# Keys in natural order, a bias band, direct value loads and a new load order in an attention and FFN kernel

## The chip, the cores and the metric

The kernel runs on one core of one Trainium2 chip. The metric is the device time of one execution in microseconds (us). Engines: PE is TensorE (matmuls), PEld its weight loads, DVE is VectorE, ACT is ScalarE, POOL is GpSimd, SP is SyncE. "SPq" and "POOLq" are the instruction streams of SyncE and GpSimd when they issue DMA transfers.

## The reference, cut to what matters

```python
B, H, S, D = 8, 8, 576, 64                       # batch, heads, sequence, head size
scores = q @ k.transpose(0, 1, 3, 2) / sqrt(D)
n      = abs(pos[:, None] - pos[None, :])
bucket = where(n < 16, n, min(16 + int(15 * log(n / 16) / log(8)), 31))   # 31 from n = 128 on
scores = scores + bias_table[bucket].transpose(2, 0, 1)
attn   = softmax(scores) @ v                     # [B, H, S, D]
x      = attn as [4608 tokens, 512]
out    = ((x @ w_a) * (x @ w_b)) @ w_out         # 512 -> 1536 -> 512
```

Inputs and output are float32. The kernel computes in bf16. The bias depends on the distance alone, and it is constant beyond a distance of 128, so `exp(score + bias)` is `exp(score)` times a factor that is 1 outside a band around the diagonal once the last bucket's bias is subtracted.

## The kernel before

The work is 32 steps of two heads each (a "pair"; four pairs make a batch). A step computes scores on TensorE, exponentiates on ScalarE, multiplies by the bias factors on VectorE, and multiplies by v on TensorE. From step 4 on, the FFN's matmuls are woven into the steps. The 512 main rows of a sequence are four blocks of 128; the last 64 rows are "tails" with loads of their own. In batches 0 and 1, TensorE transposes q and k; from batch 2 on, four DMA transposes issued by SyncE do it (QTb, KTb and two for tails). Step 8 is the first that uses KTb.

All loads that convert float32 to bf16 are issued by GpSimd, in program order. They rotate over eight semaphores, so that a load cannot be issued before the one eight places earlier has landed; in the trace each such issue waits on its own semaphore.

```python
def load4(src, dst, b, h0, h1):              # v: runs of four rows, rows permuted (p t)
    nc.gpsimd.dma_start(
        out=dst[:, 256 * h0:256 * h1].rearrange("p (h x) -> p h x", x=256),
        in_=src[b, h0:h1, 0:SM, :].rearrange("h (p t) d -> p h (t d)", t=NM))

def load_t(src, dst, b, h0, h1, natural):    # q, k: one load per block of rows
    for t in range(NM):                      # NM = 4
        rows = slice(128 * t, 128 * t + 128) if natural else slice(t, SM, NM)
        nc.gpsimd.dma_start(out=dst[...][:, t, h0:h1, :],
                            in_=src[b, h0:h1, rows, :].transpose([1, 0, 2]))

def v_in(b, h0, h1):                         # vn -> vm, which has a column of ones per head
    nc.vector.tensor_copy(out=vm[b % 2][:, h0:h1, :, 0:Dh], in_=vn[b % 2][...])

def mul(p, t):                               # bias factors for all 2 x 512 elements
    at, w = st[p]["at", t], W_sb[p % 4]
    nc.vector.tensor_tensor(out=at[:, :, :], in0=at[:, :, :],
                            in1=w[:, :, S - 1 + t:S - 1 + t - SM:-1], op=MULT)

# ... start: tails, q and k of heads 2 and 3, v, q and k of heads 4 to 7, ...
load_w(nc.gpsimd, 2); load_v(0, 4, 8); load_w(nc.gpsimd, 3)
load_w_in(0)                                 # first third of w_a and w_b
# ... end of step 0:
load_q(1, 0, 8); load_k(1, 0, 8); load_tails(1)
load_w_in(1); load_v(1, 0, 4); load_vt(1)
load_w_in(2); load_v(1, 4, 8)
load_w_out()
# ... end of step 4:
load_qkt(2)                                  # q, k and tails of batch 2
```

The softmax here doesn't subtract the row's maximum and nothing guards it: scores larger than these inputs give would overflow.

## Time and profile before

| | us |
|---|---|
| median of three runs, before the prediction | 437.79 (437.36 to 437.79) |
| span of the profiled execution | 436.25 |
| first exp of the attention (ScalarE) | 11.21 |
| last tails of batch 1 landed | 36.02 |
| first FFN matmul | 46.26 |
| w_out landed | 58.40 |
| KTb of batch 2 landed / first used | 76.4 / 84.05 |

The first two lines below are the page of the kernel before: busy time of each engine with its share of the span, and the granted TensorE clock in tenths over 40 equal slices (9 is 90% or more). The third, from the page as well, is the chain of work that ended last, by engine.

```profile
PE 418.2 (96%) x3349; PEld 206.1 (47%) x3349; DVE 235.2 (54%) x529; ACT 244.6 (56%) x346; POOL 103.5 (24%) x139
PEclk8595999999999999999999999999999999999999
PE 89%; DMA 5%; POOL 3%; DVE 2%; issue 1%; ACT 0%; DVEq 0%; POOLq 0%
```

TensorE is 96% busy, and it is 89% of the chain. Half clock lies within the first four slices (the clock records say 8.1 to 21.8 and 32.0 to 42.3 us). The next view is the busy time by window, with the columns of its first line; GB/s is what the transfers moved.

```profile
core 0: us, PE busy (x) PEld busy (x) DVE busy (x) ACT busy (x) POOL busy (x), PEclk, DMA share, GB/s
20.00:30.00 10.00, 8.97 (x134) 6.38 (x132) 8.69 (x25) 9.00 (x13) 6.62 (x8) 0.91 1.64 202
30.00:40.00 10.00, 7.01 (x61) 4.42 (x61) 3.56 (x11) 3.71 (x6) 8.59 (x13) 0.60 1.70 159
100.00:400.00 300.00, 300.00 (x2391) 145.24 (x2390) 162.51 (x348) 174.40 (x249) 37.67 (x49) 1.00 0.58 80
```

In the 300 us from 100 to 400, TensorE is busy for 300.00 us at clock 1.00. So there is little in this stretch that less VectorE work could shorten. Only the first 80 us hold idle TensorE time. The largest waits of TensorE (list of waits: line that waits, what it waited for, total us, times, longest):

```profile
PE tab_ps L221 <- DMA oh_sb<-oh_const: 3.4, 1, 3.4
PE trq L276 <- DMA qn<-in_q_dram: 2.8, 5, 0.7
```

Finally the timeline of SyncE around the transposes of batch 2, and of TensorE where step 8 begins (start, duration, then the instruction; for a DMA the duration is that of its issue):

```profile
66.29 4.74 SPq L312 DMA_TRANSPOSE KTb<-kn  x1
84.05 0.61 PE L327 MATMUL qk<-QTb,KTb 64*128 64x512 bf16 x4
```

The transpose was issued at 66.29 us and its data landed at 76.4 us. It was used at 84.05 us, without a wait. The last load of its k is the eighth after w_out in GpSimd's program:

```profile
39.10 1.07 POOL L166 DMA_DIRECT2D wo<-in_moe_w_out_dram  x1
58.93 0.89 POOL L127 DMA_DIRECT2D kn<-in_k_dram  x1 [7.17 <-PE pa L446]
```

### The profile page before, as it was taken

What the parts mean: (1) busy time and instruction counts of PE and PEld (TensorE: products, weight loads), DVE (VectorE), ACT (ScalarE), POOL (GpSimd) and SP (SyncE); (2) the same over time, 40 slices, a digit from 0 to 9 for tenths busy, and PEclk for the clock granted to TensorE, in tenths of its full rate; (3) what the DMA queues carried; (4) which work ended last, traced back from release to release, by engine and by line L of the source; (5) the groups of instructions that cost most, each with busy time, mean ns of one, the idle gap of its engine ahead of it and who ended that gap; (6) DMA issues with size and microseconds to landing.
All of it is one profiled execution on the core that took longest, in us unless ns stands there. A gap on an engine that the chain in (4) does not pass through costs nothing.

```text
span 436.2 us, 8373 instructions
## 1 busy us (share of the span) xinstructions
PE 418.2 (96%) x3349; PEld 206.1 (47%) x3349; DVE 235.2 (54%) x529; ACT 244.6 (56%) x346; POOL 103.5 (24%) x139
## 2 busy tenths in 40 slices
PE   5978998999999999999999999999999999999995
PEld 2455554554444444444545444444444454444442
DVE  3674767665764576456655575466636651321320
ACT  1875665657665666566656665666566633223321
POOL 9966547290009000720063001000000000000000
PEclk8595999999999999999999999999999999999999
DMA  9999999999249925994579562431021002002004
GB/s 125 205 177 171 200 164 188 140 130 183 52 56 109 226 41 64 90 184 101 63 63 193 106 76 38 131 73 39 15 86 38 15 20 81 0 19 79 0 4 94
DMA packets 145863, 41.87 MB, mean 96 GB/s; under 512 B 127608, under 2 KB 141080, under 8 KB 145824
## 3 DMA queue, kind: packets, MB, share of 16 engines
q0 software_dynamic: 90864, 19.21, 51.7%
q1 hardware_dynamic: 53760, 21.79, 24.2%
q8 instruction: 26, 0.43, 0.4%
q10 hardware_dynamic: 1200, 0.33, 0.4%
q14 instruction: 13, 0.11, 0.1%
HBM read 39.22 MB, written 9.45 MB: 112 GB/s over the span
## 4 chain that ended last, share of the span: by engine, by line
PE 89%; DMA 5%; POOL 3%; DVE 2%; issue 1%; ACT 0%; DVEq 0%; POOLq 0%
PE pb L456 23%; PE po L466 22%; PE pa L446 22%; PE av L400 9%; PE qk L327 7%; DMA qn<-in_q_dram 2%; PE av L391 2%; PE qkt L349 1%; DMA vt<-in_v_dram 1%; PE qkt L352 1%; POOL qn L127 1%; DMA qtl<-in_q_dram 1%; PE trx L429 1%; DVE g L459 0%; DVE at L343 0%
## 5 line engine op out<-in xcount | busy, mean ns | idle before, releaser
L338 ACT ACTIVATE at<-qk 128x1024 bf16<-128x1024 f32 x128 | 126.8, 1025 | 28.5 <-PE qk L327 28.1
L459 DVE TENSOR_TENSOR g<-pb,ha 128x512 bf16<-128x512 f32 x108 | 74.7, 692 | 102.0 <-PE pb L456 90.6
L446 PE MATMUL pa<-xn,wa 128*128 128x512 bf16 x432 | 111.1, 379 | 0.0
L456 PE MATMUL pb<-xn,wb 128*128 128x512 bf16 x432 | 110.9, 379 | 0.0
L450 ACT ACTIVATE ha<-pa 128x512 f32<-128x512 f32 x108 | 64.5, 598 | 72.6 <-PE pa L446 72.5
L466 PE MATMUL po<-wo,g 128*128 128x512 bf16 x432 | 102.5, 379 | 0.0
L343 DVE TENSOR_TENSOR at<-at,W 128x1024 bf16<-128x1024 bf16 x128 | 86.0, 685 | 9.2 <-ACT at L338 8.9
L456 PEld LDWEIGHTS <-wb 128*128 128x128 bf16 x432 | 38.8, 97 | 53.0 <-issue 17.2
L446 PEld LDWEIGHTS <-wa 128*128 128x128 bf16 x432 | 38.8, 98 | 49.8 <-issue 10.3
L466 PEld LDWEIGHTS <-g 128*128 128x128 bf16 x432 | 38.4, 98 | 45.9 <-issue 7.6
L470 ACT ACTIVATE ob<-po 128x512 f32<-128x512 f32 x36 | 21.5, 597 | 68.3 <-PE po L466 68.3
L400 PE MATMUL av<-vm,at 128*128 128x65 bf16 x1024 | 48.5, 197 | 0.2 <-DVE vm L318 0.2
L400 PEld LDWEIGHTS <-at 128*128 128x128 bf16 x1024 | 43.9, 100 | 6.9 <-issue 0.3
L408 DVE RECIPROCAL rc<-av 128x6 f32<-128x6 f32 x64 | 12.1, 189 | 46.9 <-PE av L400 44.8
L391 PE MATMUL av<-vt,att 128*128 128x130 bf16 x160 | 35.6, 223 | 0.0
L409 DVE TENSOR_TENSOR XG<-av,rc 128x384 bf16<-128x384 f32 x64 | 31.4, 491 | 2.4 <-DVE rc L408 0.2
L363 ACT ACTIVATE att<-qkt 128x1024 bf16<-128x1024 f32 x32 | 32.6, 1020 | 0.0
L127 POOL DMA_DIRECT2D kn<-in_k_dram x32 | 27.9, 907 | 12.8 <-PE pa L446 8.8
L127 POOL DMA_DIRECT2D qn<-in_q_dram x32 | 27.7, 885 | 6.4 <-PE trq L276 5.7
L327 PE MATMUL qk<-QTb,KTb 64*128 64x512 bf16 x192 | 29.1, 381 | 0.0
L120 POOL DMA_DIRECT2D vn<-in_v_dram x10 | 8.6, 857 | 70.7 <-DVE vm L318 69.2
L148 POOL DMA_DIRECT2D vt<-in_v_dram x16 | 10.0, 638 | 60.1 <-PE av L400 60.0
(79 smaller groups left out, 243.3 us busy)
## 6 DMA issues: line engine op xcount, KB each, us to landing
out_dram<-ob SPq DMA_DIRECT2D x32, 256.0 KB, 2.3
qn<-in_q_dram POOLq DMA_DIRECT2D x28, 128.0 KB, 6.6
kn<-in_k_dram POOLq DMA_DIRECT2D x28, 128.0 KB, 9.2
vn<-in_v_dram POOLq DMA_DIRECT2D x6, 512.0 KB, 6.7
wa<-in_moe_w_a_dram POOLq DMA_DIRECT2D x3, 512.0 KB, 9.3
wb<-in_moe_w_b_dram POOLq DMA_DIRECT2D x3, 512.0 KB, 10.5
wo<-in_moe_w_out_dram POOLq DMA_DIRECT2D x1, 1536.0 KB, 19.3
vn<-in_v_dram POOLq DMA_DIRECT2D x4, 256.0 KB, 7.5
```

The lines of the kernel that those rows point to most:

```text
L127: nc.gpsimd.dma_start(out=dst[b % 2][:, :].rearrange("p (t h d) -> p t h d", h=H, t=NM)[:, t, h0:h1, :], in_=src[b, h0:h1, rows, :].transp ...
L327: nc.tensor.matmul(out=ps[:, hh, :], lhsT=kT_(p, t)[r, :], rhs=qT[r, :, :], start=True, stop=True)
L338: nc.scalar.activation(out=at[:, :, :], in_=ps[:, :, :], func=ACTF.Exp, scale=scale)
L343: nc.vector.tensor_tensor(out=at[:, :, :], in0=at[:, :, :], in1=w[:, :, S - 1 + t:S - 1 + t - SM:-1], op=MULT)
L363: nc.scalar.activation(out=at[:, ST:ST + 1024].rearrange("p (a x) -> p a x", a=2), in_=ps[:, :, :], func=ACTF.Exp, scale=scale)
L391: nc.tensor.matmul(out=pav[:, slot, :, :], lhsT=x, rhs=vt[i][:, hp, :, :], start=True, stop=True)
L400: nc.tensor.matmul(out=pav[:, slot, hh, :], lhsT=x, rhs=vm[i][:, 2 * hp + hh, t, :], start=False, stop=True, skip_group_check=True)
L446: nc.tensor.matmul(out=pa[:, :], lhsT=wa_sb[df // 4][:, mc, 128 * (df % 4):128 * (df % 4) + 128], rhs=xn_sb[mc][:, 512 * c:512 * c + 512], ...
L450: nc.scalar.activation(out=ha[:, :], in_=pa[:, :], func=ACTF.Copy)
L456: nc.tensor.matmul(out=pb[:, :], lhsT=wb_sb[df // 4][:, mc, 128 * (df % 4):128 * (df % 4) + 128], rhs=xn_sb[mc][:, 512 * c:512 * c + 512], ...
L459: nc.vector.tensor_tensor(out=g_sb[df][:, :], in0=pb[:, :], in1=ff["ha"][:, :], op=MULT)
L466: nc.tensor.matmul(out=po[:, :], lhsT=g_sb[df][:, 128 * tt:128 * tt + 128], rhs=wo_sb[:, df, :], start=(df == 0), stop=(df == NDF - 1))
```

## The change

The intent is fourfold. Keys stay in natural order, so the bias differs from 1 only on a band of 384 columns; VectorE multiplies 2 x 384 or 2 x 256 elements instead of 2 x 512. Values go straight into the tile that the matmul reads, so VectorE's copies disappear; their packets shrink from 512 to 128 bytes. The first transposes are split to start the first exp earlier. The loads are cut into smaller pieces and put in the order in which they are needed. The diff, cut to its core:

```diff
-    def load_t(src, dst, b, h0, h1, natural):
+    def load_t(src, dst, b, h0, h1):
         for t in range(NM):
-            rows = slice(128 * t, 128 * t + 128) if natural else slice(t, SM, NM)
             nc.gpsimd.dma_start(
-                in_=src[b, h0:h1, rows, :].transpose([1, 0, 2]))
+                in_=src[b, h0:h1, 128 * t:128 * t + 128, :].transpose([1, 0, 2]))
+    def load_p(src, dst, b, hp):                 # q or k of one pair: one load per head
+        for h in (2 * hp, 2 * hp + 1):
+            load_h(nc.gpsimd, src, x[:, :, h, :], b, h)
+    def load_v(b):                               # all heads, one load per block of rows
+        for t in range(NM):
+            nc.gpsimd.dma_start(out=vm[b % 2][:, :, t, 0:Dh], in_=v[b, :, 128*t:128*t+128, :]...)
+    def load_vp(b, hp):                          # v of one pair: one load per head
+        for h in (2 * hp, 2 * hp + 1):
+            load_h(nc.gpsimd, v, vm[b % 2][:, h, :, 0:Dh], b, h)
 ...
     def mul(p, t):
-        nc.vector.tensor_tensor(out=at[:, :, :], in0=at[:, :, :],
-                                in1=w[:, :, S - 1 + t:S - 1 + t - SM:-1], op=MULT)
+        lo, hi = max(0, 128 * (t - 1)), min(SM, 128 * (t + 2))
+        ...
+        nc.vector.tensor_tensor(out=at[:, :, lo:hi], in0=at[:, :, lo:hi], in1=w[...], op=MULT)
 ... start:
-    load_tails(0); heads 2, 3 of q and k; load_v(0, 0, 4); load_q(0, 4, 8); load_k(0, 4, 8); load_vt(0)
-    load_w(nc.gpsimd, 2); load_v(0, 4, 8); load_w(nc.gpsimd, 3); load_w_in(0)
+    load_p(q, qn, 0, 1); load_p(k, kn, 0, 1); tails; load_vp(0, 0); load_vt(0)
+    load_p(q, qn, 0, 2); load_p(k, kn, 0, 2); load_vp(0, 1); load_w(nc.gpsimd, 2)
+    load_p(q, qn, 0, 3); load_p(k, kn, 0, 3); load_vp(0, 2); load_vp(0, 3); load_w(nc.gpsimd, 3)
 ... end of step 0:
-            load_q(1, 0, 8); load_k(1, 0, 8); load_tails(1); load_w_in(1)
-            load_v(1, 0, 4); load_vt(1); load_w_in(2); load_v(1, 4, 8); load_w_out()
+            load_t(q, qn, 1, 0, 4); load_t(k, kn, 1, 0, 4); load_tails(1); load_w_in(0)
+            load_vp(1, 0); load_vp(1, 1); load_vt(1); load_w_in(1)
+            load_t(q, qn, 1, 4, 8); load_t(k, kn, 1, 4, 8); load_vp(1, 2); load_vp(1, 3)
+            load_w_in(2); load_w_out()
 ... (start split, smaller W tiles and single tail products left out)
```

## The prediction

> **What bounds the kernel now.** From 80 us to 428 us TensorE is busy in every microsecond at granted clock 1.00 (table of busy time by window; one FFN chunk repeats every 45.1 us in the chain). VectorE (60%) and ScalarE (63%) are far from full there. So about 350 us of the 436 us span are TensorE-throughput bound, and the change leaves the matmuls of that stage as they are. Only the first 80 us can give anything. There TensorE is idle about 13 us and runs at half clock from about 8 to 22 us and from 32 to 42 us. The Trainium skill (TensorE: Matmul & The Clock Gate, Part 1) says that an idle window of about 3.4 us halves the clock; the trace agrees: the two halvings follow the wait for the one-hot constant (3.4 us, list of waits) and the waits for batch 1's first q, k and tails (29 to 36 us). The gate that counts is the second one: in step 3 the transposes for head pair 4 wait for qn (landing until 32.0), kn (35.1) and the tails (36.0); the first FFN matmul follows 10 us later, at 46.3.
>
> **What the change does, costed.**
> - Bias product on the band: 1024 elements take 685 ns, 512 take 424, so 768 about 555 ns (estimate by interpolation): 2.74 to 1.96 us per pair; tail products 0.83 to about 0.47; the v copies (16 x 0.49) go. VectorE loses about 45 us, nearly all of it off the critical path: worth 0 to 1 us, in the waits of 50 to 70 us.
> - Start: the one-hot no longer lands last, transposes are split, tail transposes leave the front. First exp at about 9.3 instead of 11.2 us. But the step-3 wait swallows this.
> - Load order: before batch 1's first k and tails, the first weight part (4.5 us of landing time: 22.4 to 26.1 and 28.3) and heads 4 to 7 of q and k no longer stand in the queue. But the loads are now 64 KB each, and GpSimd spends 0.75 us issuing one (0.9 us for 128 KB). Adding the issues in program order (28 x 0.78, 10 tail loads x 0.65, two W x 0.85, one small) the last tail of batch 1 is issued at about 30.5 us and lands at about 33 (36.0 before). The queue turns from transfer-bound into issue-bound, so most of the reordering's profit is lost.
> - v in 128-byte packets costs DMA: 1.84 instead of 1.35 us per four heads (estimate from 0.92 us per 1024 packets): not critical early; it uses up the slack of batch 2's transposed keys (landed 76.4, used 84).
>
> **On the critical path:** about 3 us at the gate, 0.5 to 1 us in steps 5 to 7, perhaps minus 0.5 us at step 8. First FFN matmul at about 43 us; from there the same TensorE-bound stream.
>
> **Predicted time: 433.9 us (before 437.8), 0.9% less; 8 in 10 for 430.0 to 437.3. Chances: faster by over 2% 0.10, within 2% 0.88, slower 0.02.**
>
> **What would show the steps right.** First exp near 9.3 us; waits for qn, kn or tails in step 3 still there, ending near 33 us, with GpSimd over 90% busy to 30 us; the clock still at half after them; VectorE 190 us busy instead of 235; from about 76 us on TensorE full, 45.1 us per chunk.
>
> **What would make it wrong.** If no stall of a window's length is left in step 3, the clock stays full and 4 to 6 us more are gained (about 428). If loads into the 130-byte-strided v tile are slow, or the many small loads land late, pairs 1 to 3 stall as well and nothing is gained. If step 8 waits for the transposed keys, the gain shrinks.

## The result and the profile after

The kernel after takes 443.1 us (median of four runs, 442.92 to 444.7) where the kernel before takes 437.58 us in the same rounds. The ratio is 1.0135, with a 95% interval of 1.011 to 1.016. The prediction was 433.9 us with a range of 430.0 to 437.3; the result lies above the range, on the other side of the kernel before.

The page of the kernel after, same three lines as above:

```profile
PE 418.2 (94%) x3349; PEld 205.3 (46%) x3349; DVE 196.3 (44%) x490; ACT 241.5 (55%) x339; POOL 133.4 (30%) x178
PEclk9988999779999999999999999999999999999999
PE 79%; DMA 11%; POOL 7%; issue 1%; ACT 0%; POOLq 0%
```

VectorE lost 39 us of work and TensorE did exactly the same 418.2 us. A caution on the clock line: it shows full clock where the trace has no record. The first record of the kernel after is at 15.6 us, and until then its matmuls of 512 columns take about 604 ns, later 387, so its first slices ran at half clock although the line begins with 9, 9. But two low slices have appeared at 77 to 100 us (the digits 7, 7), and the chain now holds 11% DMA and 7% GpSimd where it held 5% and 3%. GpSimd issues more: it went from 139 to 178 instructions and from 103.5 to 133.4 us. The waits of TensorE and the windows say where:

```profile
PE qk L322 <- DMA KTb<-kn: 8.4, 1, 8.4
```

```profile
20.00:30.00 10.00, 8.41 (x114) 5.14 (x111) 7.62 (x25) 8.47 (x11) 10.00 (x15) 0.96 1.41 104
30.00:40.00 10.00, 7.76 (x98) 5.15 (x97) 4.34 (x14) 5.22 (x7) 7.41 (x11) 0.70 1.23 139
79.00:84.00 5.00, 0.97 (x6) 0.24 (x3) 0.82 (x4) 0.18 (x1) 4.32 (x5) 0.99 2.04 151
84.00:94.00 10.00, 5.66 (x39) 2.90 (x40) 1.08 (x3) 2.54 (x3) 5.08 (x7) 0.50 2.04 154
100.00:400.00 300.00, 300.00 (x2431) 145.61 (x2430) 136.45 (x324) 175.78 (x249) 57.05 (x72) 1.00 0.78 83
```

From 79 to 84 us TensorE is busy for 0.97 of 5 us, and then, from 84 to 94 us, the clock stands at 0.50. TensorE waits 8.4 us in one piece for KTb of batch 2, and pays a second time for the wait with the clock. The timelines show that the transpose came late because its input came late:

```profile
77.22 5.15 SPq L314 DMA_TRANSPOSE KTb<-kn  x1
88.34 1.03 PE L322 MATMUL qk<-QTb,KTb 64*128 64x512 bf16 x4 [8.38 <-DMA KTb<-kn]
```

The transpose is issued at 77.22 us instead of 66.29, and lands at 88.30 instead of 76.4. Most of the 10.9 us is the k load, which landed at 75.71 instead of 66.14; for the last 1.3 us SyncE was still issuing QTb's transpose (72.47 to 77.05). Three intervals of the two profiled executions add up to the whole difference:

| interval | before | after | difference |
|---|---|---|---|
| start to first FFN matmul | 46.26 | 42.39 | -3.87 |
| first FFN matmul to step 8's first matmul | 37.79 | 45.95 | +8.16 |
| step 8's first matmul to the end | 352.20 | 354.58 | +2.38 |
| span | 436.25 | 442.92 | +6.67 |

The gain of 3.9 us at the start was there, as predicted. The second line is mostly the wait of 8.4 us. The third fits the half clock after it: 5.8 us of it (88.34 to 94.11) fall behind step 8's first matmul, and with 604 instead of 387 ns for a matmul of 512 columns about 2.1 us of them are lost (an estimate from these figures). (The profiled execution of the kernel after is its slowest, 444.7 us; the other three are at 443.0, so the profile overstates the loss by some 1.6 us.)

### Why the keys were late

GpSimd's own timeline of the kernel after (in brackets its idle time and what the profile says ended it):

```profile
53.06 1.09 POOL L164 DMA_DIRECT2D wo<-in_moe_w_out_dram  x1
69.01 0.87 POOL L122 DMA_DIRECT2D kn<-in_k_dram  x1 [7.28 <-DMA wo<-in_moe_w_out_dram]
```

The last load of batch 2's k is the eighth after w_out, and could not be issued before w_out (1536 KB in bf16) had landed. It was the same in the kernel before, where w_out was issued at 39.10 and landed at 58.40, and the last k load was issued at 58.93. (There the timeline names a matmul of TensorE as the releaser; but the issue came 0.5 us after w_out's landing, as in the kernel after, where w_out is named.) So the late keys follow a late w_out: +10.1 us for its landing (58.40 to 68.49), +9.6 us for the landing of the last k load (66.1 to 75.7), +10.9 us for the issue of the transpose.

The 10.1 us can be followed through the landings, which the trace gives for each load. The new order moved the first weight part (it landed from 22.4 to 28.3 us, 5.9 us) and heads 4 to 7 of batch 1's q and k (half of 6.8 us, 3.4 us) from before the gate (the last tails of batch 1) to behind it. That is about 9.3 us of transfers. If nothing else had changed, the gate would have opened 9.3 us earlier, and w_out would have landed when it did. Two things were lost:

- The gate opened only 3.4 us earlier (36.02 to 32.62). That loses 5.9 us. The window from 20 to 30 us shows why: GpSimd is busy for 10.00 of 10 us, and the transfers move 104 GB/s where they moved 202. Loads of 64 KB (bf16) are issued every 0.73 us, and the time from issue to landing shrinks from 4.1 us (the first q load of batch 1) to 3.0 (the last k load before the gate): the transfers catch up with the issuing. Where 16 such loads stand in a row (r6 below), the last ten land 0.72 us apart, as they are issued. When such loads are queued up instead (at 48 to 51 us in the trace of the kernel after), they land every 0.44 us. So they were limited by the issuing, not by the transfers.
- From the gate to w_out's landing, 35.9 us pass instead of 22.4. That is 13.5 us more, while only 9.3 us of transfers were moved there, so 4.2 us are lost. V of batch 1 takes 5.4 us instead of 3.3, which is 2.1 of them. The weights take the other 2.0: two halves of weight parts (512 KB each) were issued less than 2 us before the last small load ahead of them had landed, and as a half lands some 6 us after its issue (6.05 and 6.12 us), each took 4.2 us of the queue; in the kernel before the same two halves took 3.6 and 2.3. That is 2.4 us; the rest of the weights came 0.4 us faster.

5.9 and 4.2 make the 10.1 us. This is a reading of two traces. The experiments test it.

### The profile page after: what moved, and what is told of

The parts are those of the page before. It is cut to its first block, busy times and chain, and to the rows that moved or that the text cites. A ratio compares the mean times of both kernels' runs of the same rounds, so it can differ in the third digit from the quotient of the medians. Undisturbed runs are those within 1.5% of the kernel's fastest.

```text
span 442.9 us, 8382 instructions
## 1 busy us (share of the span) xinstructions
PE 418.2 (94%) x3349; PEld 205.3 (46%) x3349; DVE 196.3 (44%) x490; ACT 241.5 (55%) x339; POOL 133.4 (30%) x178
## 4 chain that ended last, share of the span: by engine, by line
PE 79%; DMA 11%; POOL 7%; issue 1%; ACT 0%; POOLq 0%
PE po L458 21%; PE pb L448 20%; PE pa L438 19%; PE av L392 7%; PE qk L322 6%; DMA wb<-in_moe_w_b_dram 4%; DMA kn<-in_k_dram 4%; DMA KTb<-kn 2%; POOL vm L127 2%; PE av L383 2%; POOL qn L122 1%; DMA vt<-in_v_dram 1%; PE qkt L347 1%; PE qkt L350 1%; POOL kn L122 1%
## 5 line engine op out<-in xcount | busy, mean ns | idle before, releaser
L458 PE MATMUL po<-wo,g 128*128 128x512 bf16 x432 | 104.1, 384 | 0.0
L341 DVE TENSOR_TENSOR at<-at,W 128x512 bf16<-128x512 bf16 (+1 forms) x128 | 60.3, 483 | 10.8 <-ACT at L333 10.7
L438 PEld LDWEIGHTS <-wa 128*128 128x128 bf16 x432 | 38.8, 98 | 49.8 <-issue 10.5
L136 POOL DMA_DIRECT2D vm<-in_v_dram x24 | 21.1, 893 | 107.9 <-PE av L392 106.8
L383 PEld LDWEIGHTS <-att 128*128 128x128 bf16 x160 | 16.0, 100 | 8.9 <-issue 1.8
```

The lines of the kernel that those rows point to most:

```text
L341: nc.vector.tensor_tensor(out=at[:, :, lo:hi], in0=at[:, :, lo:hi], in1=w[:, :, y:(None if z < 0 else z):-1], op=MULT)
L383: nc.tensor.matmul(out=pav[:, slot, :, :], lhsT=x, rhs=vt[i][:, hp, :, :], start=True, stop=True)
L438: nc.tensor.matmul(out=pa[:, :], lhsT=wa_sb[df // 4][:, mc, 128 * (df % 4):128 * (df % 4) + 128], rhs=xn_sb[mc][:, 512 * c:512 * c + 512], ...
L458: nc.tensor.matmul(out=po[:, :], lhsT=g_sb[df][:, 128 * tt:128 * tt + 128], rhs=wo_sb[:, df, :], start=(df == 0), stop=(df == NDF - 1))
```

## The experiments

Theory A: cutting loads into many small pieces makes GpSimd's issuing the limit, the weights fall behind, and batch 2's keys, which stand behind all of the weights in the same queue, come too late. Rivals: B, the order is to blame, whatever the pieces; C, the 128-byte packets of v are to blame; D, the other parts (band, split start) cost time of their own. Two more questions: what are the band and the split start worth, and is there a version that beats both kernels?

All runs below were timed against the kernel before on the same chip. Its median was 437.96 (r1, r2, r3, r5), 437.68 (r6 to r9) and 437.99 us (r10 to r12). All results are correct except r3. There is no r4 on record.

| kernel | us, median (range) | ratio to before (95%) | tails of batch 1 land | w_out lands | step 8's first matmul |
|---|---|---|---|---|---|
| before | 437.58 (437.23 to 437.79) | | 36.0 | 58.4 | 84.05 |
| after | 443.1 (442.92 to 444.7) | 1.0135 (1.011 to 1.016) | 32.6 | 68.5 | 88.34 |
| r1, w_out later | 441.23 (439.04 to 441.69) | 1.0069 (1.0041 to 1.0098) | 32.4 | 83.1 | 87.19 |
| r2, old order | 442.05 (441.71 to 442.67) | 1.0100 (1.0084 to 1.0115) | 41.2 | 65.4 | 88.97 |
| r3, v in long runs | 440.27 (438.95 to 441.16) | 1.0051 (1.0024 to 1.0078) | 31.7 | 66.5 | 85.48 |
| r5, batch 1 in whole pieces | 436.61 (436.31 to 437.16) | 0.9975 (0.996 to 0.999) | 34.5 | 63.2 | 82.88 |
| r6, r5's order in small pieces | 447.13 (446.24 to 447.62) | 1.0217 (1.0201 to 1.0232) | 38.2 | 70.3 | 90.51 |
| r7, fewer issues | 437.26 (435.75 to 438.49) | 0.9992 (0.9967 to 1.0017) | 33.0 | 62.2 | 82.35 |
| r8, v of batch 2 later | 437.47 (435.71 to 438.72) | 0.9995 (0.9968 to 1.0022) | 32.9 | 62.3 | 82.37 |
| r9, r7 with products doubled | 440.45 (439.56 to 441.4) | 1.0071 (1.0049 to 1.0093) | 33.1 | 62.6 | 83.26 |
| r10, r7 with keys before w_out | 433.07 (432.86 to 433.23) | 0.9890 (0.9874 to 0.9907) | 33.4 | 75.1 | 79.25 |
| r11, r10 with the band undone | 435.16 (434.59 to 435.22) | 0.9934 (0.9919 to 0.9949) | 33.1 | 76.3 | 80.87 |
| r12, r10 with the start unsplit | 432.66 (431.98 to 433.35) | 0.9880 (0.9864 to 0.9896) | 33.7 | 75.1 | 79.76 |

### r1: w_out moved behind the keys

```diff
 # end of step 0
             load_w_in(2)
-            load_w_out()
 # end of step 4
             load_qkt(2)
+            load_w_out()
```

> The changed kernel, with the load of the output weights (1.5 MB in bf16, 8 us of landing time) issued behind batch 2's q, k and tails and not in front of them. Theory 1 (the loss is the one wait at step 8 for the transposed keys of batch 2, 8.4 us, plus the half clock of 10.2 us that follows it): the last k of batch 2 lands about 8 us earlier (near 68 instead of 75.7 us), the transposed keys near 80 instead of 88.3, the wait falls under 1 us, the clock stays full, time 430.5 to 433.5 us. Rival (something else in the changed kernel costs time too, for example slower work after step 8): the wait goes, but the time stays above 436 us.

Measured: 441.23 us. The wait for KTb is gone, and another stands in its place:

```profile
PE po L458 <- DMA wo<-in_moe_w_out_dram: 5.4, 1, 5.4
```

The expectation missed. W_out, issued at 66.2 us, landed at 83.1 us and was needed at about 77.7; TensorE waited 5.4 us for it and ran at half clock from 80.4 to 87.2 us. Also, the issue of KTb's transpose took 10.2 us beside w_out instead of 5.15, so the keys landed at 86.15 us, only 2 us earlier. So it is not the place of one load alone: the whole queue is some 10 us behind, and one of the two must wait.

### r2: the order of before, v in the pieces of after

```diff
+    load_tails(0)                                   # in front again
-    load_p(q, qn, 0, 2); load_p(k, kn, 0, 2) ... pair 3
+    load_t(q, qn, 0, 4, 8); load_t(k, kn, 0, 4, 8)
+    load_w_in(0)                                    # end of the start, before batch 1
 # end of step 0
-            load_t(q, qn, 1, 0, 4); load_t(k, kn, 1, 0, 4); load_tails(1); load_w_in(0)
+            load_t(q, qn, 1, 0, 8); load_t(k, kn, 1, 0, 8); load_tails(1); load_w_in(1)
             load_vp(1, 0); load_vp(1, 1); load_vt(1)
-            load_w_in(1); load_t(q, qn, 1, 4, 8); load_t(k, kn, 1, 4, 8)
+            load_w_in(2)
```

> The changed kernel's work (natural keys, band products, v straight into its tile, split first transposes), with the load order of the kernel before: tails first, first weight part before batch 1, batch 1's q and k in whole pieces. Theory 1a (the order made the keys late): the step-8 wait is under 2 us and the time 434 to 438 us, near the kernel before, with the step-3 wait back near 36 us. Rival 1b (v's four times as many packets made them late): the wait at step 8 stays over 4 us and the time over 440 us.

Measured: 442.05 us. The wait for KTb is gone, as expected, but the loss of time is not, which the expectation missed: the wait has moved to the gate in step 3.

```profile
PE trq L276 <- DMA qn<-in_q_dram: 7.2, 4, 5.2
```

The tails of batch 1 land at 41.2 us, 5.2 us later than in the kernel before, with the kernel before's order of the loads. The kernel still loads v in single heads and in short packets: eight v loads stand before the gate instead of two, and six more issues of 0.73 us are 4.4 us (an estimate). So B falls as the whole explanation: with the old order restored the queue is still late, and only the place of the wait differs.

### r3: v in long runs again (wrong values on purpose)

The number and the places of the loads stay; v is read in 1 KB runs into its old tile and copied by VectorE. Since keys are now in natural order, v no longer matches them, and the result is wrong (relative error 0.136). Only the time counts.

```diff
-    load_h(nc.gpsimd, v, vm[b % 2][:, h, :, 0:Dh], b, h)      # 128-byte packets
+    load4(b, h, h + 1)                                        # 512-byte packets into vn
+    nc.vector.tensor_copy(out=vm[...], in_=vn[...])           # every second step
```

> The changed kernel in its own order and with the same number of v loads, but each v load in long runs (1 KB read, 512 bytes written) into a staging tile, copied by VectorE as before; the values are wrong on purpose (v rows stand in another key order than the weights). Rival 1b (packet count of v): transposed keys at least 4 us earlier than 88.3, wait at step 8 under 4.5 us, time under 439 us. Theory 1a (order): at most 3 us earlier (an estimate from 0.46 against 0.34 us per head, 24 heads), wait still over 5 us, time 439.5 to 443 us.

Measured: 440.27 us; KTb lands 2.9 us earlier (85.4 instead of 88.3) and TensorE still waits 7.9 us for it, since the first FFN matmul came earlier as well (40.04 us). So C is real and small: v's packets cost about 2.8 us of the 443.1 (by the ratios to the kernel before 0.8%, or 3.7 us, and VectorE's copies are back in this run), near what the landings gave above (2.1 us for batch 1), and they don't explain a wait of 8 us.

### r5 and r6: the same order in large and in small pieces

Both load all of batch 1's q and k before the first weight part. They differ only in the pieces of batch 1.

```diff
 # end of step 0; r5 against after
-            load_t(q, qn, 1, 0, 4); load_t(k, kn, 1, 0, 4)   ... heads 4 to 7 behind load_w_in(1)
+            load_t(q, qn, 1, 0, 8); load_t(k, kn, 1, 0, 8)   # 8 loads of 128 KB
             load_tails(1); load_w_in(0)
-            load_vp(1, 0); load_vp(1, 1)                     ... pairs 2, 3 behind
+            load_v(1)                                        # 4 loads of 128 KB
             load_vt(1); load_w_in(1); load_w_in(2); load_w_out()
 # r6 against r5
-            load_t(q, qn, 1, 0, 8); load_t(k, kn, 1, 0, 8)
+            load_t(q, qn, 1, 0, 4); load_t(q, qn, 1, 4, 8)   # 16 loads of 64 KB
+            load_t(k, kn, 1, 0, 4); load_t(k, kn, 1, 4, 8)
-            load_v(1)
+            for hp in range(4): load_vp(1, hp)               # 8 loads of 64 KB
```

> The changed kernel with batch 1's q, k and v in whole pieces of eight heads (12 issues of 128 KB instead of 24 of 64 KB), the second half of q and k moved with the first. Rival 1c (GpSimd's issue time and the limit of eight loads under way starve the DMA engines, because the pieces are small): output weights land 4 us or more earlier than 68.5, wait at step 8 under 5 us, time under 440 us, although the step-3 wait grows by 2 to 4 us. If pieces do not matter: output weights land within 1.5 us of 68.5, wait over 7 us.

> The order of the run with batch 1 in whole pieces, but with the pieces cut to 64 KB again (24 issues instead of 12): tells the order from the size. Theory 1c (issues and the limit of eight loads under way): output weights land after 67 us (63.2 with whole pieces), transposed keys at 86 us or later, time over 440 us. Rival (only the order of that run helped): output weights within 1.5 us of 63.2, time 436 to 438 us.

Measured: 436.61 and 447.13 us, 10.5 us apart, from the size and number of the pieces alone, and both as theory A expected: TensorE waits 0.8 us for KTb in r5 and 4.5 us in r6, which also waits longer at the gate (tails at 38.2 against 34.5 us). (They ran on two chips; the kernel before differed by 0.3 us between them, and the ratios to it are 0.9975 and 1.0217.) GpSimd's timeline of r5, where x4 means four loads in a row, with the window from 30 to 40 us of the same run:

```profile
22.22 3.60 POOL L122 DMA_DIRECT2D qn<-in_q_dram  x4
25.72 3.60 POOL L122 DMA_DIRECT2D kn<-in_k_dram  x4
44.40 1.02 POOL L164 DMA_DIRECT2D wo<-in_moe_w_out_dram  x1
```

```profile
30.00:40.00 10.00, 8.21 (x75) 5.02 (x75) 3.94 (x11) 4.05 (x5) 8.81 (x12) 0.55 1.59 160
```

And of r6, with the same window:

```profile
22.14 6.01 POOL L122 DMA_DIRECT2D qn<-in_q_dram  x8
28.02 6.05 POOL L122 DMA_DIRECT2D kn<-in_k_dram  x8
51.26 1.07 POOL L164 DMA_DIRECT2D wo<-in_moe_w_out_dram  x1
```

```profile
30.00:40.00 10.00, 3.19 (x25) 1.74 (x26) 1.36 (x3) 0.91 (x1) 10.00 (x16) 0.51 1.21 86
```

The same bytes of q and k take 7.1 us to issue in r5 and 11.9 us in r6. In r6 GpSimd is busy for 10.00 of 10 us, the transfers move 86 GB/s, and TensorE, short of keys, is busy for 3.19 us. W_out is issued 6.9 us later and lands 7.2 us later. This is theory A. The Trainium skill (DMA: Bandwidth & Descriptors, Rules for kernel authors) advises to coalesce small transfers and says that under 64 KB one pays mostly overhead; these traces agree with the advice, with loads of 64 and 128 KB (bf16), so that the limit of 64 KB itself is not tested; and they show that the overhead here is the issuing engine's time.

r5 alone, which is the change with batch 1 in large pieces, is already 6.5 us faster than the change and a little faster than the kernel before. The change's own order is not to blame: with the same small pieces r6, which loads all of batch 1's q and k first, is 4 us slower than the change.

### r7 and r8: fewer issues still, and v of batch 2 later

```diff
 # r7 against r5
-    load_w(nc.sync, 1)
+    for hp in range(1, 4): load_w(nc.sync, hp)      # bias tables of pairs 2, 3 off GpSimd
-    load_vp(0, 0); load_vt(0) ... load_vp(0, 1) ... load_vp(0, 2); load_vp(0, 3)
+    load_v(0); load_vt(0)                           # 4 loads of 128 KB, before pair 3's q and k
 # r8 against r7
+            if b == 2: load_v(b); load_vt(b)        # end of step 6, before load_qkt(3)
-            if s % 4 == 0:
+            if s % 4 == 0 and b > 2:
```

> Batch 1 in whole pieces, batch 0's v in four pieces of 128 KB instead of eight of 64 KB, and the tables of head pairs 2 and 3 issued by the sync engine and not by GpSimd: some 4.7 us less of GpSimd issuing before batch 1. Theory 1c: the tails of batch 1 land near 30.5 us (34.5 with whole pieces only), the first FFN matmul near 40.5 us, output weights near 59, transposed keys near 78, hardly any wait at step 8, time 432 to 434 us, faster than both kernels. Rival (transfers, not issues, set the pace): the landings move by less than 1.5 us and the time stays within 1 us of 436.6.

> The run before, with batch 2's v loaded two steps later, so that it doesn't run beside the transposes of batch 2's q and k. If these loads delay the transposes: the transposed keys land 2 us or more after issue sooner (10 us instead of 12) and a rest of the step-8 wait goes (0 to 1 us of time). Otherwise the same as the run before within 0.7 us.

Measured: 437.26 and 437.47 us. In r7 the gate is mended: between 27.66 us and step 8 the clock is full (r5: half from 28.7 to 38.9), and the first FFN matmul comes at 41.8 us (44.5 in r5). The start is not: the clock records of r7 begin only at 27.66 us, and the page shows full clock before it, but TensorE's timeline shows half, 0.61 us for two matmuls and then 0.39:

```profile
26.90 0.61 PE L318 MATMUL qk<-QT,KT 64*128 64x512 bf16 x2
28.14 0.39 PE L318 MATMUL qk<-QT,KT 64*128 64x512 bf16 x2
```

But the expected 432 to 434 us were missed, because the keys came no earlier than in r5 (first use 82.35 against 82.88 us):

```profile
PE qk L318 <- DMA KTb<-kn: 3.0, 1, 3.0
```

```profile
62.78 0.87 POOL L122 DMA_DIRECT2D kn<-in_k_dram  x1 [6.40 <-DMA wo<-in_moe_w_out_dram]
```

From the tails' landing at 33.0 to w_out's at 62.2 us the queue now only transfers weights and v, and the last k load still stands behind w_out. Fewer issues can't help there. The earlier first FFN matmul just turned into a longer wait at step 8.

r8 was an empty experiment. Its v loads were to be issued later, but between their old and new place in GpSimd's program no other load stands, and GpSimd does not wait for the steps of the other engines. The trace has them at 67.45 us, against 67.39 in r7. So whether v's loads beside the transposes delay KTb is not answered by any run here. It shows only that the medians of two programs with equal load times agree within 0.2 us, while each one's runs spread over some 3 us.

### r9: every band product done twice

r7 and, after each band product, a product with ones on the same columns. The result stays correct; VectorE gets about 60 us more work.

```diff
+        nc.vector.tensor_tensor(out=at[:, :, lo:hi], in0=at[:, :, lo:hi],
+                                in1=one_sb[:, :, 0:hi - lo], op=MULT)
```

> The few-issues kernel with every band product followed by one of the same size with ones (results unchanged), so VectorE does about 60 us more, more than the band saves. If VectorE is off the critical path, as predicted: within 1.5 us of the few-issues kernel. If the band's saving counts: slower by more than 4 us.

Measured: 440.45 us, 3.2 us more than r7. The expectation was up to 1.5 us if VectorE is off the critical path and over 4 if the band's saving counts; the result lies between. The waits of TensorE:

```profile
PE trx L421 <- DVE XG L401: 3.5, 5, 1.3
PE pb L448 <- DVE g L451: 3.1, 13, 0.6
```

VectorE's load is thus not free: with 60 us more, 3.2 us show in the time, as short waits for XG (the normalized attention) and g (the FFN's product), though VectorE was far from full on average. It does not add up by shares of busy time: a product that runs just when the next result is needed delays it.

### r10: keys before w_out, on top of fewer issues

```diff
 # r10 against r7: the same two lines as in r1
-            load_w_out()          # end of step 0
             load_qkt(2)
+            load_w_out()          # end of step 4
```

> The few-issues kernel with batch 2's q, k and tails issued in front of the output weights. In the run that only moved the output weights, they landed at 83.1 us, 5.4 us too late for step 7; here all loads stand some 6 us earlier. If the bytes in front of batch 2's keys are what is left of the step-8 wait: transposed keys near 76 to 78 us (82.3 in the few-issues run), output weights near 73 to 76, before their first use near 77, no wait at step 8, clock full, time 431.5 to 434 us, faster than both kernels. If the transposes and the output weights slow each other as they did in that earlier run (a transpose took 17 us from issue to landing): a wait of over 2 us for one of them stays, time 435 to 437 us.

Measured (five rounds): 433.07 us, ratio 0.9890 to the kernel before. This beats both kernels. In r1 the same edit only exchanged one wait for another; here the queue is some 6 us less behind (w_out at 62.2 us in r7, at 68.5 in the change), so both loads are in time. W_out lands at 75.1 us and is first used at 77.15, and KTb is used at 79.25 without a wait:

```profile
PEclk9999999999999999999999999999999999999999
62.62 8.47 SPq L310 DMA_TRANSPOSE KTb<-kn  x1
79.25 0.61 PE L318 MATMUL qk<-QTb,KTb 64*128 64x512 bf16 x4
```

The clock line is 9 throughout, but as in r7 its first record is at 27.2 us, and up to there the matmuls run at half clock (604 ns for 512 columns, 387 after). From then on no half clock is recorded until after the last matmuls (430 us). From step 8 to the end it takes 351.8 us, as the kernel before did (352.2), so the whole gain lies before step 8.

### r11 and r12: what are the band and the split start worth?

r11 puts back 27.2 us of VectorE work in r10 (products with ones, on the two of four blocks whose band is 256 columns), close to the 24.3 us that the band took away from these products (86.0 before; 35.0 and 26.7, together 61.7, after). r12 does r10's first transposes whole, as the kernel before did.

```diff
 # r11 against r10
+        if t in (0, 3):
+            nc.vector.tensor_tensor(out=at[:, :, lo:hi], in0=at[:, :, lo:hi],
+                                    in1=one_sb[:, :, :], op=MULT)
 # r12 against r10
-    t32(psk, k32, 0); t32(psq, q32, 0); t32(psq, q32, 1); first copies; t32(psq, q32, 2) ...
+    for t in range(NM): t32(psq, q32, t)
+    for t in range(NM): t32(psk, k32, t)
+    copy(ACT, QT[0][:, :], psq[:, :]); copy(None, KT[0][:, 0:SM], psk[:, :])
```

> The keys-first kernel with an added product by ones in the first and last key block of each pair, 0.85 us a pair or 27 us in all, about what the band saves on VectorE (results unchanged). If the band's saving is worth nothing where TensorE sets the pace: within 1 us of the keys-first kernel. If it is worth something (doubling all products cost 3.2 us, half of it in the first steps): 1 to 2.5 us slower.

> The keys-first kernel with the first transposes of pair 0 in two whole groups, as in the kernel before. If the step-3 wait for batch 1's tails swallows what the split saves at the start: first exp 0.5 to 1.5 us later, first FFN matmul within 0.5 us, time within 0.7 us of the keys-first kernel. If the start counts: slower by as much as the first exp is later.

Measured: r11 takes 435.16 us, 2.1 us more than r10. In the profile 1.2 us of it lie before the first FFN matmul and 0.7 us after step 8. So 27 us of VectorE work cost about 2 us here, and that is an estimate of what the band is worth in a queue that isn't late; the products were not put back in their old form. r12 takes 432.66 us, and its range holds r10's. Its first exp even starts earlier (7.91 against 9.46 us; its clock was full from 4.4 to 7.8 us, so the two starts do not compare cleanly), but it gains nothing either, since step 1's wait for v's tails takes it all:

```profile
PE av L379 <- DMA vt<-in_v_dram: 6.4, 1, 6.4
```

In r10 that wait is 3.0 us. No gain of the split start is seen in these runs, and rival D falls for both parts: neither costs time.

## Why the prediction was wrong, point by point

- **What bounds the kernel: right.** TensorE is full from 100 to 400 us in both kernels, and only the first 80 us and step 8 differ.
- **VectorE: right in size.** 196.3 us busy (190 predicted, 235.2 before). The products took what was estimated; a grouping by shape shows it (busy us, mean ns), 549 ns for 768 elements where 555 was estimated. The first line is the kernel before:

```profile
L343 DVE TENSOR_TENSOR at<-at,W 128x1024 bf16<-128x1024 bf16 x128 | 86.0, 685 | 9.2 <-ACT at L338 8.9 <-DMA W<-bias_tab 0.3
L341 DVE TENSOR_TENSOR at<-at,W 128x768 bf16<-128x768 bf16 x64 | 35.0, 549 | 7.8 <-ACT at L333 7.8
L341 DVE TENSOR_TENSOR at<-at,W 128x512 bf16<-128x512 bf16 x64 | 26.7, 417 | 3.0 <-ACT at L333 2.9
```

- **What that saving is worth: probably too small.** 0 to 1 us was predicted; r11 lets one estimate about 2 us.
- **Start: right.** First exp at 9.38 us (9.3 predicted), and the wait of step 3 swallows it, as predicted. r12 shows no gain from the split itself.
- **Gate: right.** The last tails of batch 1 landed at 32.6 us ("about 33"), GpSimd was busy throughout to 30 us, the first FFN matmul came at 42.39 us ("about 43"), and the clock was at half around the gate (29.3 to 36.1 us).
- **The step that failed:** "it uses up the slack of batch 2's transposed keys (landed 76.4, used 84)" and "perhaps minus 0.5 us at step 8". The slack was 7.7 us, and step 8's need moved forward by the 3.9 us gained. The keys landed 11.9 us later, where 7.7 - 3.9 = 3.8 us of slack were left, and TensorE waited 8.4 us. The term that was mis-sized is the delay of the queue at batch 2's keys. The prediction charged it with the packets of v, and had noticed that the queue was issue-bound, but followed that only as far as the gate. It did not carry the lost transfer time on to w_out and the keys, which are later in the same queue: 5.9 us before the gate and 4.2 us behind it. (It also wrote 4.5 us for the first weight part, where its own numbers, 22.4 to 28.3, give 5.9.)
- **The chances: the likeliest case came, on the other side.** It gave 0.88 to a change within 2%, and 1.35% slower is within 2%.
- **The clock: told as a rule, not applied here.** A wait of 8.4 us holds two idle windows of 3.4 us (the Trainium skill, TensorE: Matmul & The Clock Gate, Part 1). The trace agrees: the clock stood at half from 83.9 to 94.1 us, and step 8 to the end took 2.4 us more. But it also halves without an idle window: at 29.26 us in the kernel after, when TensorE had been busy for 2.13 of the 3.41 us before and never idle for more than 0.57 us at a time, and at 32.03 us in the kernel before (0.98 of 3.41 us, at most 0.72 idle at a time). So the prediction's "the trace agrees" fits the first halving, and the one at the gate only roughly. The prediction listed a wait at step 8 among what could make it wrong, but said that the gain would shrink; it did not reckon that it would turn into a loss.

What the experiments settle: the same order in small and large pieces is 10.5 us apart (r5, r6); the old order does not save the change (r2); v's packets are 2.8 us (r3); moving w_out alone does not either (r1); fewer issues and the keys before w_out together give 433.07 us (r10), which is close to what was predicted for the change. What stays open: whether v's loads beside batch 2's transposes delay these (r8 did not test it), and what another order of the weights would give.

## What to carry to other kernels

A queue of loads that one engine issues in order has two limits, the engine's issue time per load and the transfer time, and cutting loads into smaller pieces trades the second for the first; compare the two for each size in the trace before cutting. When a change delays or reorders such a queue, follow the delay to the last load that has a deadline, not only to the first gate that it should open, because time in which the queue ran below its rate is lost for everything behind. And a long wait of TensorE can be paid twice, here with 8.4 us and then with half clock to 94.1 us, so a shortage of slack (here some 8 us) can turn a gain into a loss.

## What the Trainium skill lacked or had wrong

- **DMA: Bandwidth & Descriptors** (Issuing engines are not separate DMA queues) calls the sequencer's time to initiate a DMA "usually small relative to the DMA itself", and (Anatomy of one DMA) the descriptor generation "small, variable". For GpSimd's converting loads here it is not small: 0.73 us for each load of 64 KB (bf16), which is transferred in 0.44 us when queued up, and 0.87 us for 128 KB, which takes 0.92. Only larger loads pay little (a half of a weight part, 512 KB: 0.74 to 0.95 us against about 2.6).
- **TensorE: Matmul & The Clock Gate** (Part 1) says that the clock returns after at least one busy window of about 3.4 us, but not how busy a window must be. In the kernel before it stayed at half for 13.7 us (8.1 to 21.8) while TensorE was busy for 8.45 of the 10 us from 10 to 20. After step 8's wait it took 10.2 us, of which TensorE worked from 88.34 on. The traces give a measure. The recorded changes of the clock lie multiples of 3.41 us apart (13.65 and 10.24 in the kernel before). Each of the 33 recorded rises in the 13 profiles follows 3.41 us in which TensorE was busy for at least 2.97 us (3.41 at 21.8 and at 42.3 us in the kernel before), and no recorded stretch of this length that stayed at half had more than 3.03. So it took about 3 of 3.41 us here.
